# Linear attention with a highway layer: sums of two batches moved earlier, x copies on ScalarE, x added on GpSimd for three of four blocks

## The chip, the cores and the metric

The kernel runs on one core of a Trainium2 chip. The core has five engines that each work through a queue of their own: TensorE (matrix products; PE in the profile, its weight loads PEld), VectorE (DVE), ScalarE (ACT), GpSimd (POOL) and SyncE (SP, which here issues all the transfers). They wait for one another through semaphores. The metric is the time of one execution on the device, in microseconds (us); less is better. "Before" is the kernel without the change, "after" the one with it.

## The reference

Two layers in a row. The first is linear attention on 8 batches of 8 heads, 576 positions and 64 features: q goes through a softmax over its features, k through a softmax over the positions, and the output is q's softmax times the 64x64 matrix of k's softmax times v. The second is a highway layer with 512 features on the 4608 rows (batch times position) that come out.

```python
def _attn_ref(q, k, v):                       # each (8, 8, 576, 64)
    q_s = softmax of q over axis -1
    k_s = softmax of k over axis 2
    kv = np.einsum('bhsd,bhse->bhde', k_s, v)
    return np.einsum('bhsd,bhde->bhse', q_s, kv)

x = attn_out.transpose(0, 2, 1, 3).reshape(4608, 512)

def _moe_ref(x, w_h, w_t, b_t):
    H = np.maximum(x @ w_h, 0.0)
    T = 1.0 / (1.0 + np.exp(-(x @ w_t + b_t)))
    return T * H + (1.0 - T) * x
```

## The kernel before

**Tiles.** A batch's q, k and v are loaded as 128 partitions x 4 head pairs x 9 position groups x 64 features in fp32. The 9 groups are split as 4 + 4 + 1 where transposes are concerned; eight of the nine make a "row block" of 512 columns, and the ninth groups of all batches are gathered in `x9` for the end.

**The chain of a batch b.** ScalarE takes the exponential of q and of k, each in two halves (`exp_half`, line 170). VectorE sums q's exponential over the features, in two halves (`q_sums`, line 225), and takes the reciprocal (`q_recip`, line 243). GpSimd multiplies the exponential by it (`q_scale_p`, line 255, tile `eq`), in two parts, and casts v to fp16 (`cast_v`, line 182). TensorE transposes the scaled q (`q_trans`, line 67, tile `pq`; copied to SBUF as `qsT` by VectorE, line 272) and multiplies k by v in two halves (`kv_half`, tile `psk`); v carries a column of ones, so that k's sums come out beside it. VectorE divides by these sums (`kv_norm`, lines 212 and 214, tile `kvn`). TensorE then makes x, the attention's output in transposed form (`x_pair`, tile `px`, four blocks of 128 features), and ScalarE or VectorE copies it to SBUF as `xT` (lines 295 and 297). The ninth group goes its own way (`x_left`, line 310).

**The highway layer of a row block c** (c = b; blocks 8 and 9 are the two halves of `x9`) has four output blocks `ob`. For each, TensorE makes the gate's product (`gate`, tile `pt`), on which ScalarE puts a tanh (line 332), and the carry product (`carry`, tile `ph`, with half the weight less the identity). VectorE makes `dd` (line 350) and the blend `g` (`blend`, line 358). Then x has to be added. For blocks in `added(g)` GpSimd does it (`add_x`, line 367); for the others TensorE does it for nothing but its own time, by transposing x into the same PSUM tile as `g`, in `turn_block`. An output tile (`out_tile`, tile `nat`) turns one position group of two row blocks, g = c // 2, back into rows: for each of four feature blocks one matmul with `g` as the weights, and one more with `xT` where GpSimd didn't add. ScalarE copies it (line 397), and SyncE stores four tiles at a time (line 400).

**What sets the order.** The kernel is scheduled by hand. The list at the end (line 515) gives the order of the start. After it, each piece of work is entered with a due time by `at(p, ...)`, where a row block takes 8 units, and all pieces are emitted in the order of their times; pieces with the same time, in the order of entry. Each engine keeps the order in which its instructions were emitted. Batch b's preparation stands in row block b - 1 (p = 8 * (b - 1)) and, for the exponential and the sums of q, in the block before that one. The numbers in lines 477 to 511 are what the change touches:

```python
    for b in range(2, B):
        p = 8 * (b - 1)
        ...
        for i in range(3):
            at(p + tr[i], E(q_trans, b, i))
        at(p + kv[0], E(kv_half, b, 0))
        at(p + kv[1], E(kv_half, b, 1), E(kv_norm, b))
        at(p + x[0], E(x_pair, b, 0))
```

**Buffers.** PSUM has four tiles for `pt` and `ph`, three (`ps_q`) for `pq`, `psk` and `px`, and one for `nat`. SBUF has two of each exponential, three of `xT`, two of `g`, three of each loaded tensor.

Of the kernel before, what the change touches and what calls it, by code (L numbers as in the profile page):

```python
# [18 lines left out]
def kernel(  # L19
# [10 lines left out]
    nc = tc.nc  # L30
# [3 lines left out]
    N9 = S // 64  # L34
# [239 lines left out]
    def x_pair(b, a, even=False, home=None):  # L274
        ps, tag = home or (ps_q, "qx")
        g, b2 = b // 2, b % 2
        if a == 0 and b2 == 0:
            xT[g] = xtp.tile([P, 4, NM, 2, 64], FP16, tag="xT", name=f"xT_{g}")
        t = [
            ps.tile([P, NM, 64], FP32, tag=tag, name=f"px_{b}_{a}_{c}")  # L280
            for c in range(2)
        ]
        for x in range(2):
            for c in range(2):
                r = slice(64 * c, 64 * c + 64)
                mm(
                    t[c][64 * x : 64 * x + 64].rearrange("p n d -> p (n d)"),
                    kvn[b % 2][r, x, a, :],
                    qsT[b][r, 2 * a + x, 0:NM, :].rearrange("p n d -> p (n d)"),
                    True, True,  # L290
                )
        for c in range(2):
            dst = xT[g][:, 2 * a + c, :, b2, :]
            if (c == 0) if even else (a + c < 2):
                nc.scalar.copy(dst, t[c])  # L295
            else:
                nc.vector.tensor_copy(dst, t[c])  # L297
# [62 lines left out]
        )  # L360


    added = lambda g: (0, 1) if g < 3 else (0, 1, 2)

    def add_x(c, ob):
        xv, gv = views(c)
# [71 lines left out]
    def at(p, *fs):  # L438
        events.setdefault(p, []).extend(fs)

    E = lambda f, *a: (lambda: f(*a))

    for c in range(1, B + 2):
        for ob in range(4):
            p = 8 * c + 2 * ob
# [6 lines left out]
    for g in range(B // 2):  # L452
        p = 16 * (g + 1)
# [6 lines left out]
    p = 8 * B + 8  # L460
# [10 lines left out]
    at(14.5, E(add_x, 1, 1))  # L471
    for c in range(2, B):
        for ob in added(c // 2):
            at(8 * c + 2 * ob + 2.5, E(add_x, c, ob))
    at(11, E(cast_v_head, 2, 2, nc.gpsimd), E(cast_v_head, 2, 3, nc.scalar))
    at(11, E(q_scale_p, 2, 8, N9))
    for b in range(2, B):
        p = 8 * (b - 1)
        if b > 2:
            s = p + {3: -2, 4: -4}.get(b, -5)  # L480
            at(s, E(exp_half, b, "q", 0))
            at(s + 1, E(exp_half, b, "q", 1))
            if b > 3:
                at(s + 1, E(q_sums, b, 0))
                at(s + (3.5 if b == 4 else 2), E(q_sums, b, 1), E(q_recip, b))
            else:
                at(s + 2.5, E(q_sums, b, 0))
                at(s + 3.5, E(q_sums, b, 1), E(q_recip, b))
            if b > 3:
                at(s + (3.6 if b == 4 else 2), E(q_scale_p, b, 0, 4))  # L490
                at(s + (3.7 if b == 4 else 3), E(q_scale_p, b, 4, N9))
            s = p + {3: 0, 4: 0}.get(b, -1)
            at(s, E(exp_half, b, "k", 0))
            at(s + 1, E(exp_half, b, "k", 1))
            s -= 2 if b == 4 else 0
            at(s, E(cast_v, b, 0))
            at(s + 1, E(cast_v, b, 1))
            if b == 3:
                at(p + 1.6, E(q_scale_p, b, 0, 4), E(q_scale_p, b, 4, N9))
        tr, kv, x = {  # L500
            2: ((5, 6, 6.4), (4, 6.2), (7, 7.5, 7.6)),
            3: ((4.5, 5.5, 6), (3, 4), (6.5, 7, 7.5)),
            4: ((2, 3, 4), (4, 5), (6, 6, 7)),
        }.get(b, ((2, 3, 4), (3, 4), (5, 6, 7)))
        for i in range(3):
# [4 lines that stand above are left out]
        at(p + x[1], E(x_pair, b, 1))  # L510
        at(p + x[2], E(x_left, b))
    for b in range(4, B):
        at(8 * (b - 3), *[E(load, b, w) for w in "qkv"])

    for f in [
        E(warm_up, 20),
        E(exp_half, 0, "q", 0), E(q_sums, 0, 0),
        E(exp_half, 0, "q", 1), E(q_sums, 0, 1),
        E(q_recip, 0), E(q_scale_v, 0, 0, 4), E(q_scale_v, 0, 4, N9),
        E(exp_half, 0, "k", 0), E(cast_v, 0, 0),  # L520
        E(exp_half, 0, "k", 1), E(cast_v, 0, 1),
        E(q_trans, 0, 0), E(q_trans, 0, 1), E(warm_up, 2), E(q_trans, 0, 2),
        E(warm_up, 6),
        E(kv_half, 0, 0), E(gate_bias), E(warm_up, 2), E(kv_half, 0, 1), E(kv_norm, 0),
        *[E(cast_weight, "t", k_, (nc.vector, nc.gpsimd)[k_ % 2]) for k_ in range(4)],
        E(warm_up, 4),
        E(x_pair, 0, 0), E(warm_up, 2), E(x_pair, 0, 1), E(warm_up, 1), E(x_left, 0),
        E(exp_half, 1, "q", 0), E(q_sums_tree, 1, 0),
        E(exp_half, 1, "q", 1), E(q_sums_tree, 1, 1), E(q_recip, 1),
        E(less_one, 0), E(cast_weight, "h", 0, nc.scalar, 0.5),  # L530
        E(less_one, 1), E(cast_weight, "h", 1, nc.gpsimd, 0.5),
        E(less_one, 2), E(cast_weight, "h", 2, nc.scalar, 0.5),
        E(less_one, 3), E(cast_weight, "h", 3, nc.scalar, 0.5),
        E(q_scale_p, 1, 0, 4), E(q_scale_p, 1, 4, 8),
        E(gate, 0, 0), E(gate, 0, 1), E(gate, 0, 2, (ps_q, "qx")), E(warm_mid, 5),
        E(carry, 0, 0), E(blend, 0, 0), E(carry, 0, 1), E(exp_half, 1, "k", 0),
        E(gate, 0, 3, (ps_nat, "nat")), E(blend, 0, 1), E(carry, 0, 2),
        E(q_trans, 1, 0), E(blend, 0, 2), E(carry_products, 0, 3),
        E(exp_half, 1, "k", 1),
        *[E(cast_v_head, 1, c, (nc.scalar, nc.gpsimd, nc.gpsimd, nc.scalar)[c]) for c in range(4)],  # L540
        E(q_scale_p, 1, 8, N9),
        *[E(load, 2, w) for w in "qk"], E(load, 2, "v", [nc.sync, nc.sync]),
        *[E(load, 3, w) for w in "qkv"],
        E(q_trans, 1, 1), E(kv_half, 1, 0), E(kv_half, 1, 1), E(kv_norm, 1),
        E(q_trans, 1, 2), E(carry_diff, 0, 3), E(exp_half, 2, "q", 0),
        E(x_pair, 1, 0, True), E(x_pair, 1, 1, True, (ps_ht, "ht")),
        E(q_sums_tree, 2, 0), E(exp_half, 2, "q", 1), E(q_sums_tree, 2, 1), E(q_recip, 2),
    ]:
        f()
# [33 lines left out]
```

The softmax here doesn't subtract the row's maximum and nothing guards it: scores larger than these inputs give would overflow.

## Time and profile before

| | |
|---|---|
| median of 5 runs | 136.52 us (135.57 to 136.84) |
| the profiled execution: its time, its span | 136.79 us, 134.9 us |
| TensorE busy | 116.0 us, 86% of the span |
| VectorE busy | 104.6 us, 78% |
| ScalarE busy | 90.7 us, 67% |
| GpSimd busy | 71.2 us, 53% |
| granted TensorE clock | 0.999 |
| read from HBM, written | 30.41 MB, 9.44 MB |

The page cuts the span into 40 slices of 3.4 us, each digit the busy share in tenths:

```profile
PE   4949996897798698787797999899989999999960
DVE  1395638599998798978599788988998775779880
ACT  3651256989955798569669869796975566566630
POOL 2006419960399929966934983499089632430000
DMA  4999999999999999984999399993007004227874
```

The first six slices are the start: batch 0 is loaded and goes through its chain. From about 43 us on (slice 13) the blocks follow each other: row block 2 has its gates from 46 us, block 3 from 60, block 4 from 74, block 5 from 86, block 6 from 98, block 7 from 110. TensorE is nearly always busy there[...]. The end, from 118 us on, has no attention left: blocks 8 and 9 and the last tiles.

### The profile page before, as it was taken

The page shows a single profiled execution, that of the slowest core. Times are in us where ns is not written, and L with a number is a line of the kernel's source. Part 1 is how long each engine was busy: PE and PEld are TensorE (multiplying, and loading weights), DVE is VectorE, ACT ScalarE, POOL GpSimd, SP SyncE. Part 2 cuts the span into 40 slices and gives each one's busy share as a digit, 9 for nine tenths or more (in the row PEclk, how much of TensorE's full clock was granted, in tenths as well). Part 3 has the DMA queues.
Part 4 walks back from the last instruction along what each step waited for, and adds up shares of the span by engine and source line. Part 5 has one row for each costly group of instructions (what it writes and reads, how often), then busy time and mean ns, then how long its engine had stood idle before and what let it go on. Part 6 is the DMA issues. An engine that isn't in the chain of part 4 may idle for free.

```text
span 134.9 us, 3493 instructions
## 1 busy us (share of the span) xinstructions
PE 116.0 (86%) x1427; PEld 64.5 (48%) x1427; DVE 104.6 (78%) x209; ACT 90.7 (67%) x134; POOL 71.2 (53%) x65
## 2 busy tenths in 40 slices
PE   4949996897798698787797999899989999999960
PEld 1425341362354255444452564456446555589950
DVE  1395638599998798978599788988998775779880
ACT  3651256989955798569669869796975566566630
POOL 2006419960399929966934983499089632430000
PEclk9999999999999999999999999999999999999999
DMA  4999999999999999984999399993007004227874
GB/s 140 374 389 373 412 402 411 412 412 410 406 413 400 412 411 415 401 334 177 279 411 410 151 281 401 404 422 134 0 0 316 2 0 199 117 95 323 357 313 160
DMA packets 15847, 40.06 MB, mean 297 GB/s; under 512 B 724, under 2 KB 1240, under 8 KB 14808
## 3 DMA queue, kind: packets, MB, share of 16 engines
q1 hardware_dynamic: 15832, 39.85, 76.6%
q8 instruction: 11, 0.18, 0.5%
q14 instruction: 4, 0.03, 0.1%
HBM read 30.41 MB, written 9.44 MB: 295 GB/s over the span
## 4 chain that ended last, share of the span: by engine, by line
PE 43%; DVE 20%; ACT 9%; POOL 8%; DMA 8%; SPq 6%; issue 3%; DVEq 0%; ACTq 0%; POOLq 0%
PE pt L62 14%; PE ph L62 12%; DMA w32h<-in_moe_w_h_dram 8%; PE nat L62 6%; POOL eq L255 6%; PE pq L67 4%; DVE r L225 4%; DVE dd L350 4%; SPq L94 4%; DVE g L358 3%; PE psk L62 3%; ACT pt L332 3%; ACT ek L170 3%; DVE xT L297 2%; SPq L109 2%
## 5 line engine op out<-in xcount | busy, mean ns | idle before, releaser
L255 POOL TENSOR_TENSOR eq<-eq,r 128x1024 f16<-128x1024 f16 (+2 forms) x16 | 29.7, 1875 | 17.6 <-DVE r L243 11.0
L332 ACT ACTIVATE pt<-pt,bt 128x512 f32<-128x512 f32 (+1 forms) x40 | 24.7, 622 | 21.2 <-PE pt L62 21.2
L62 PE MATMUL pt<-xT,w16t 128*128 128x512 f16 x128 | 33.4, 380 | 2.2 <-DVE xT L297 0.9
L62 PE MATMUL ph<-xT,w16h 128*128 128x512 f16 x128 | 33.3, 380 | 1.5 <-ACT w16h L114 1.0
L350 DVE SCALAR_TENSOR_TENSOR dd<-xT,ph 128x512 f16<-128x512 f16 x32 | 21.9, 684 | 7.4 <-PE ph L62 6.5
L358 DVE SCALAR_TENSOR_TENSOR g<-pt,dd 128x512 f16<-128x512 f32 (+1 forms) x40 | 25.0, 627 | 2.3
L367 POOL TENSOR_TENSOR g<-g,xT 128x512 f16<-128x512 f16 x18 | 20.5, 1153 | 9.3 <-DVE g L358 9.3
L170 ACT ACTIVATE eq<-q 128x1152 f16<-128x1152 f32 x16 | 18.5, 1171 | 4.5 <-DMA q<-in_q_dram 4.5
L62 PEld LDWEIGHTS <-w16t 128*128 128x128 f16 x160 | 14.1, 98 | 14.4 <-issue 3.2
L62 PEld LDWEIGHTS <-w16h 128*128 128x128 f16 x160 | 13.7, 98 | 12.7 <-ACT w16h L114 2.2
L170 ACT ACTIVATE ek<-k 128x1152 f16<-128x1152 f32 x16 | 18.5, 1171 | 1.6 <-DMA k<-in_k_dram 1.6
L225 DVE TENSOR_REDUCE r<-eq 128x18 f32<-128x1152 f16 x12 | 16.2, 1346 | 3.8 <-ACT eq L170 3.7
L182 POOL CAST v<-v 128x1152 f16<-128x1152 f32 x12 | 13.5, 1148 | 9.9 <-DMA v<-in_v_dram 9.9
L295 ACT CAST xT<-px 128x512 f16<-128x512 f32 x23 | 12.8, 594 | 7.8 <-PE px L62 7.8
L397 ACT COPY o<-nat 128x512 f32<-128x512 f32 x28 | 16.6, 594 | 1.9 <-PE nat L62 0.9
L62 PE MATMUL nat<-ident,g 128*128 128x128 f16 x142 | 17.6, 219 | 0.2
L62 PEld LDWEIGHTS <-g 128*128 128x128 f16 x144 | 13.7, 98 | 7.8 <-issue 1.4
L67 PE MATMUL pq<-ident,eq 128*128 128x128 f16 x144 | 12.0, 219 | 5.7 <-POOL eq L255 2.9
L272 DVE COPY qsT<-pq 128x1024 f16<-128x1024 f16 (+1 forms) x24 | 13.2, 554 | 3.6 <-PE pq L67 3.3
L67 PEld LDWEIGHTS <-eq 128*128 128x128 f16 x144 | 9.2, 98 | 9.7 <-POOL eq L255 4.1
L62 PE MATMUL warm<-wide,ident 128*128 128x512 f16 x37 | 10.6, 429 | 1.8 <-DVE wide L151 1.8
L62 PE MATMUL nat<-ident,xT 128*128 128x128 f16 x56 | 9.7, 219 | 0.0
(50 smaller groups left out, 104.4 us busy)
## 6 DMA issues: line engine op xcount, KB each, us to landing
out_dram<-o SPq DMA_DIRECT2D x8, 1024.0 KB, 5.1
q<-in_q_dram SPq DMA_DIRECT2D x7, 1152.0 KB, 13.8
k<-in_k_dram SPq DMA_DIRECT2D x7, 1152.0 KB, 13.2
v<-in_v_dram SPq DMA_DIRECT2D x5, 1152.0 KB, 13.7
v<-in_v_dram SPq DMA_DIRECT2D x6, 576.0 KB, 11.8
q<-in_q_dram SPq DMA_DIRECT2D x2, 576.0 KB, 4.0
k<-in_k_dram SPq DMA_DIRECT2D x2, 576.0 KB, 6.9
w32t<-in_moe_w_t_dram SPq DMA_DIRECT2D x1, 1024.0 KB, 10.7
```

What stands on the lines that cost most here:

```text
L62: mm = lambda o, l, r, st, sp: nc.tensor.matmul(o, l, r, start=st, stop=sp, skip_group_check=True)
L67: nc.tensor.matmul(o, i, ident, is_transpose=True, start=True, stop=True, skip_group_check=True,)
L170: nc.scalar.activation(dst[b][:, :, 2 * a : 2 * a + 2, :], in32[which][b][:, 2 * a : 2 * a + 2].rearrange("p c n d -> p n c d"), AF.Exp,)
L182: (eng or nc.gpsimd).tensor_copy(o, i)
L225: nc.vector.reduce_sum(qsum[b][:, :, h], eq[b][:, :, h, :], axis=AX.X)
L255: nc.gpsimd.tensor_mul(e, e, r.broadcast_to(list(e.shape)))
L272: nc.vector.tensor_copy(qsT[b][:, :, n0:n1, :], t[:, :, 0:w, :])
L332: nc.scalar.activation(ps, ps, AF.Tanh, bias=bt2[:, ob : ob + 1], scale=0.5)
L350: nc.vector.scalar_tensor_tensor(dd, xv(ob), -0.5, ps, op0=ALU.mult, op1=ALU.max)
L358: nc.vector.scalar_tensor_tensor(gv(ob), th, 1.0, dd, op0=ALU.add, op1=ALU.mult)
L367: nc.gpsimd.tensor_add(gv(ob), gv(ob), xv(ob))
L397: nc.scalar.copy(o, flat(t))
```

## The change

It moves work between engines and along the order, in five places:

- **x copies.** For batches 3 to 7, the fourth block of x is copied to SBUF by ScalarE, like the other three; before, VectorE copied it (5 copies).
- **x added.** For the row blocks 2 to 5, GpSimd adds x for three of the four feature blocks; before, for two. TensorE's output tiles of these rows take five matmuls each, not six (16 fewer in all). The third addition is emitted at 8 c + 7.4, which on GpSimd is behind the scaling of batch c + 2 and ahead of its v.
- **Start.** The second quarter of the carry weight is cast by ScalarE, not by GpSimd, so ScalarE casts all four.
- **Batches 3 and 4.** The exponential of q, its sums, and its scaling come up to a unit and a half earlier. For batch 3 the first half of q is ahead of the tanh of row block 1's last gate on ScalarE, the first sum is ahead of that block's last carry on VectorE, the scaling stands between the two halves of v on GpSimd, and the first transposes come ahead of the second half of k times v. For batch 4 the exponential is ahead of the third tanh of row block 2, the sums are ahead of that block's third carry and third blend, and the scaling is ahead of v.
- **Batches 5 to 7.** The order of exponentials and sums stays; v is emitted half a unit later, behind the third addition.

On each engine the instructions come to: VectorE five fewer, ScalarE six more, GpSimd three more, TensorE 16 matmuls and their weight loads fewer. SyncE's order of transfers is the same.

```diff
-            if (c == 0) if even else (a + c < 2):
+            if (c == 0) if even else (b > 2 or a + c < 2):
                 nc.scalar.copy(dst, t[c])
...
-    added = lambda g: (0, 1) if g < 3 else (0, 1, 2)
+    added = lambda g: (0, 1, 2) if g else (0, 1)
...
         for ob in added(c // 2):
-            at(8 * c + 2 * ob + 2.5, E(add_x, c, ob))
+            at(8 * c + (2.5, 4.5, 7.4)[ob], E(add_x, c, ob))
...
         if b > 2:
-            s = p + {3: -2, 4: -4}.get(b, -5)
-            at(s, E(exp_half, b, "q", 0))
-            at(s + 1, E(exp_half, b, "q", 1))
-            if b > 3:
-                at(s + 1, E(q_sums, b, 0))
-                at(s + (3.5 if b == 4 else 2), E(q_sums, b, 1), E(q_recip, b))
-            else:
-                at(s + 2.5, E(q_sums, b, 0))
-                at(s + 3.5, E(q_sums, b, 1), E(q_recip, b))
-            if b > 3:
-                at(s + (3.6 if b == 4 else 2), E(q_scale_p, b, 0, 4))
-                at(s + (3.7 if b == 4 else 3), E(q_scale_p, b, 4, N9))
-            s = p + {3: 0, 4: 0}.get(b, -1)
-            at(s, E(exp_half, b, "k", 0))
-            at(s + 1, E(exp_half, b, "k", 1))
-            s -= 2 if b == 4 else 0
-            at(s, E(cast_v, b, 0))
-            at(s + 1, E(cast_v, b, 1))
-            if b == 3:
-                at(p + 1.6, E(q_scale_p, b, 0, 4), E(q_scale_p, b, 4, N9))
+            e0, e1, s0, s1, sc = {
+                3: (-2.6, -1.6, -1.1, -0.1, 1),
+                4: (-5.5, -4.5, -3.7, -2.7, -2.6),
+            }.get(b, (-5, -4, -3.9, -2.9, -2.8))
+            at(p + e0, E(exp_half, b, "q", 0))
+            at(p + e1, E(exp_half, b, "q", 1))
+            at(p + s0, E(q_sums, b, 0))
+            at(p + s1, E(q_sums, b, 1), E(q_recip, b))
+            at(p + sc, E(q_scale_p, b, 0, 4), E(q_scale_p, b, 4, N9))
+            s = p + {3: 0, 4: 0}.get(b, -0.5)
+            at(s, E(exp_half, b, "k", 0), E(cast_v, b, 0))
+            at(s + 1, E(exp_half, b, "k", 1), E(cast_v, b, 1))
         tr, kv, x = {
...
-            3: ((4.5, 5.5, 6), (3, 4), (6.5, 7, 7.5)),
+            3: ((4, 5, 5), (3, 4), (6, 7, 7)),
...
-        E(less_one, 0), E(cast_weight, "h", 0, nc.scalar, 0.5),
-        E(less_one, 1), E(cast_weight, "h", 1, nc.gpsimd, 0.5),
-        E(less_one, 2), E(cast_weight, "h", 2, nc.scalar, 0.5),
-        E(less_one, 3), E(cast_weight, "h", 3, nc.scalar, 0.5),
+        *[f for k_ in range(4) for f in (E(less_one, k_), E(cast_weight, "h", k_, nc.scalar, 0.5))],
```

## The prediction

> **What bounds the kernel now.** I read the page's head first: the span is 134.9 us, the profiled run took 136.79 us, so 1.9 us lie around it. No engine is saturated over the span, so the busy shares say little; the waits of TensorE say where it loses time. From the waits (engine and line, what it waited for: us in all, times, longest):
> ```profile
> POOL eq L255 <- DVE r L243: 11.0, 3, 4.0
> PEld L67 <- POOL eq L255: 4.1, 4, 1.3
> PE pq L67 <- POOL eq L255: 2.9, 4, 0.8
> PE px L62 <- ACT xT L295: 1.3, 2, 0.9
> PE pt L62 <- DVE xT L297: 0.9, 2, 0.4
> ```
> GpSimd's scaling of the exponentials (eq, line 255) waits for VectorE's reciprocal, and TensorE's transposes (pq) wait for the scaling. The page's groups give what the change buys on GpSimd:
> ```profile
> L255 POOL TENSOR_TENSOR eq<-eq,r 128x1024 f16<-128x1024 f16 (+2 forms) x16 | 29.7, 1875 | 17.6 <-DVE r L243 11.0
> L367 POOL TENSOR_TENSOR g<-g,xT 128x512 f16<-128x512 f16 x18 | 20.5, 1153 | 9.3 <-DVE g L358 9.3
> L182 POOL CAST v<-v 128x1152 f16<-128x1152 f32 x12 | 13.5, 1148 | 9.9 <-DMA v<-in_v_dram 9.9
> ```
> TensorE's timeline says where the waits lie (start, us, operation, idle before it):
> ```profile
> 63.94 0.62 PE L67 MATMUL pq<-ident,eq 128*128 128x128 f16 x8 [0.84 <-POOL eq L255]
> 66.23 0.62 PE L67 MATMUL pq<-ident,eq 128*128 128x128 f16 x8 [0.81 <-POOL eq L255]
> ...
> 87.05 0.38 PE L62 MATMUL pt<-xT,w16t 128*128 128x512 f16 x1 [0.43 <-DVE xT L297]
> ...
> 99.29 0.38 PE L62 MATMUL pt<-xT,w16t 128*128 128x512 f16 x1 [0.43 <-DVE xT L297]
> ...
> 101.56 0.28 PE L62 MATMUL nat<-ident,g 128*128 128x128 f16 x2
> ```
> Batch 4's scaling costs TensorE two waits near 65 us; then VectorE's copy of x costs 0.43 us a batch; from 77 us on a batch takes 12.25 us, nearly all of it TensorE work. GpSimd beside it:
> ```profile
> 98.26 4.19 POOL L255 TENSOR_TENSOR eq<-eq,r 128x1024 f16<-128x1024 f16 x2 [3.63 <-DVE r L243]
> 102.40 2.24 POOL L182 CAST v<-v 128x1152 f16<-128x1152 f32 x2
> 104.60 2.26 POOL L367 TENSOR_TENSOR g<-g,xT 128x512 f16<-128x512 f16 x2
> ```
> Here GpSimd is in the scaling of batch 7 until 102.4, while TensorE starts the output tile of rows 4/5 (nat) at 101.56. Today that tile needs no GpSimd result that comes after the scaling.
>
> [...]
>
> **The change, part by part.** (Steps back to back: x copy on VectorE 0.60, on ScalarE 0.50; sum 1.26; add 1.13; scaling 1.90+2.29; v half 1.10; gate or carry product 0.87, 0.97 after 64-row matmuls; transpose 0.056.)
>
> *Start.* One weight cast (1.49 us) leaves GpSimd, where it held up two subtractions; ScalarE casts four quarters from 21.33 at 0.53 each, so to 23.46 instead of 24.22 us. The last quarter of the weight lands at about 21.6 and is subtracted by 22.2, in time. Everything behind (tanh, carry, batch 1's and 2's chains) comes 0.75 us sooner. GpSimd's own scaling at 23.56 waits for a reciprocal and gains nothing; it isn't last. Loads have landed: q3 at 38.9, needed at 39; v3 by 45.7 at the latest, needed before 47.
>
> *Batch 3.* Its exponential goes ahead of the last tanh, into ScalarE's 1.9 us gap before 41.0; its first sum fills VectorE's gap near 43. The second follows the copies of x leftovers: 45.6 to 46.9, reciprocal 47.25 (before 50.75), scaling 47.4 to 51.6. But the second half of v now stands behind the scaling: to 52.7, so the second half of k'v, which could start at 51.55, waits 1.15 us. Then VectorE has the normalisation, a sum of batch 4, a carry and the transposed copy in a row, and x waits 0.55 us more, to 56.4. The block ends where it would with the start's gain alone (gates of row block 3 at 58.95 instead of 59.66, -0.7): batch 3's old waits (0.42, 0.81) are traded for these.
>
> *Batch 4.* Exponentials behind the first output copy, from 50.5; sums at 53.9 and 56.5, reciprocal 58.15 (before 61.81), scaling 58.3 to 62.5. TensorE reaches the transposes at 62.25 and 63.55: both waits go, 2.0 us. v4, behind the scaling and one add, is done at 64.7 and 65.8; needed 65.3 and 66.7. SyncE's order is the same; batch 6's loads stand behind the first output store, which waits for ScalarE's copy of the fourth tile, 0.9 us sooner. Fewer VectorE copies give 0.15 more. Gain here: recip of batch 5 at 69.85 instead of 72.62, -2.77.
>
> *x copies.* Five leave VectorE (batches 3 to 7, 5 x 0.60), five come to ScalarE (5 x 0.50), where they end before the gate's last matmul needs them: the two 0.43 us waits go. They stand ahead of the exponential of k, which has over 2 us of slack.
>
> *Adds.* Four more on GpSimd (4.5 us), 16 x-transposes fewer on TensorE (16 x 0.056 = 0.9, of which some half are hidden by waits below). The new third add of a block stands behind the next-but-one batch's scaling and ahead of its v. This price I take from GpSimd's order:
> - Block 3: reciprocal 69.85 + 0.17 + 4.19 + 1.13 = 75.3; the output tile of rows 2/3 could start at 74.2. Wait 1.05.
> - Batch 6: reciprocal 83.75 (before 85.86); scaling, add, first half of v: 90.3; TensorE is ready at 88.6. Wait 1.75 (against before's block, which had 0.2 us to spare).
> - Block 5: reciprocal of batch 7 at 96.85 (before 98.10); scaling and add to 102.3; TensorE reaches the tile at 99.65. Wait 2.65.
>
> Behind each waiting tile stand the next transposes and carry product, ScalarE's copy of the tile, and behind that the next exponential of q, so nothing runs ahead. The transposes of batch 7 follow at 102.5; before they started at 101.89. So the whole lead of 2.8 us is spent and 0.6 is lost; the seven tiles after it win back 7 x 0.056 = 0.4. From 102 to 118 us TensorE has no gap today, and the end isn't touched. Sum: +0.2 us on the profiled 136.79, that is 137.0. The median of the runs shown is 136.52, 0.27 lower, so I put the forecast at 136.7 on their scale.
>
> Unknown costs: an x copy more on ScalarE could make nothing late or cost 0.1 us a batch (0 to +0.5, I take 0). A hop from GpSimd to TensorE shows 0.06 us; three of them at up to 0.2 make +0.4 at most, and a wait cannot gain (0). GpSimd beside VectorE: its add was 1.15 us in every place, so 0. Batch 3's two new waits come out of my sums over eight steps: from 0 (both hidden, -1.7) to double (+1.7); I take 1.7 as worked out.
>
> **The rivals.**
> *Faster: batch 3's waits don't come.* If the half of v is cast in time and the sums find room, x of batch 3 starts at 54.7 instead of 56.4, and the lead of every reciprocal behind it grows by 1.7: 135.0 us. For it: the scaling is 3.5 us sooner, and VectorE idles 0.4 and 0.8 us near 44 in this trace. Against: GpSimd's order puts v behind the scaling, which is fixed.
> *Slower: GpSimd's loop decides from batch 5 on, and the lead isn't there.* From reciprocal to reciprocal a batch now takes 4.36 (hop and scaling) + 1.13 + 1.1 + 2.3 (k'v and what lies between) + 4.3 (normalisation to reciprocal) = 13.1 us, against 12.25. That loop and the last tile cost 3.3 us in all, whatever happens before. If a load binds the start (k2 lands at about 33.0 and would be needed at 33.9, so from 0.9 us later on), its 0.75 is gone: 137.5; if batch 3's order costs another 0.9 as well, 138.4. For it: the DMA engines are at nine tenths until 57 us. Against: of v1 to v4 only v2 was waited for here.
> *Slower, by the clock.* [...]
>
> **How the numbers follow.** I give the forecast (gain and loss cancel, 136.0 to 137.4) 0.38, the faster rival 0.28, the loop without the lead 0.28 and the clock 0.06. What this kernel's measurement can tell from no change is about 0.5%, 0.7 us. So faster 0.28, same 0.38, slower 0.34. The range 134.9 to 138.3 leaves out a tenth on either side; the forecast's own is 136.0 to 137.4.
>
> **What would show it.** Right: waits of the nat loads for the add (L367) of about 1.0 and 2.6 us, one of k'v for v (L182) near 1.7 us, none of pq for eq after 60 us; reciprocals of batches 5, 6 and 7 earlier by 2.8, 2.1 and 1.3 us; carry products starting 0.75 us sooner. Wrong: nat tiles that don't wait (then the lead stays and it is near 134), or a reciprocal of batch 5 less than 2 us sooner (then slower).

## The result, and the profile after

The kernel with the change takes 138.63 us in the median of 21 runs (137.09 to 140.39), the kernel before 136.56 us in the median of 40 runs. The ratio of comparable runs is 1.010, with an interval of 1.0075 to 1.013: about 1% slower. (Executions more than 1.5% above the fastest of the same kernel are left out of ratios as disturbed; here that takes out part of what the change does, so the medians of all runs stand further apart, at 1.015.) On the scale of 136.52 the ratio gives 137.9 us, inside the predicted range of 134.9 to 138.3; the medians of all runs would give 138.6, just outside it. The forecast itself, 136.7 us and no change, was too low by 1.2 us.

The runs of after are not one cluster. Beside each time stands TensorE's mean granted clock in that execution:

| mean granted clock | runs | time, us |
|---|---|---|
| 0.998 to 1.0 | 7 | 137.09 to 137.39, and 137.8 |
| 0.984 to 0.986 | 5 | 138.16 to 139.01 |
| 0.971 to 0.975 | 9 | 139.17 to 140.39 |

So after costs 0.5% at full clock (a mean of 0.998 to 1.0), and up to 2.8% otherwise. First the full clock: the profiled run (137.8 us, span 136.1 us, clock 0.998) is one of these, and the slowest of them. In its waits (engine and line, what it waited for: us in all, times, longest) the waits for the scaling are all but gone and waits for the third addition and for v have come:

```profile
POOL eq L255 <- DVE r L243: 14.9, 6, 3.9
...
PE nat L62 <- POOL g L367: 3.2, 2, 2.4
PE psk L62 <- POOL v L182: 3.0, 2, 1.6
...
PE pt L62 <- ACT xT L295: 1.6, 1, 1.6
...
PEld L67 <- POOL eq L255: 0.3, 1, 0.3
```

The page's groups: GpSimd has four more additions, at the same duration each, and ScalarE 28 copies of x; TensorE's busy time fell from 116.0 to 114.3 us.

```profile
L367 POOL TENSOR_TENSOR g<-g,xT 128x512 f16<-128x512 f16 x22 | 25.1, 1155 | 8.9 <-DVE g L358 8.9
...
L295 ACT CAST xT<-px 128x512 f16<-128x512 f32 x28 | 15.2, 595 | 8.8 <-PE px L62 8.7
```

TensorE's timeline (start, us, operation, idle before it) puts the new waits in their places:

```profile
32.03 1.08 PE L62 MATMUL pt<-xT,w16t 128*128 128x512 f16 x4 [1.59 <-ACT xT L295]
...
52.59 0.48 PE L62 MATMUL psk<-v,ek 64*64 64x65 f16 x36 [1.45 <-POOL v L182]
...
56.32 0.41 PE L62 MATMUL px<-qsT,kvn 64*64 64x512 f16 x4 [0.53 <-DVE qsT L272]
...
75.42 0.23 PE L62 MATMUL nat<-ident,g 128*128 128x128 f16 x1 [0.81 <-POOL g L367]
...
90.59 0.48 PE L62 MATMUL psk<-v,ek 64*64 64x65 f16 x36 [1.58 <-POOL v L182]
...
102.63 0.23 PE L62 MATMUL nat<-ident,g 128*128 128x128 f16 x1 [2.42 <-POOL g L367]
...
102.81 0.61 PE L67 MATMUL pq<-ident,eq 128*128 128x128 f16 x8
```

And GpSimd's, beside the last of them. Where the tile of rows 4/5 needed nothing after the scaling before, it now waits for the addition that follows it:

```profile
97.28 4.19 POOL L255 TENSOR_TENSOR eq<-eq,r 128x1024 f16<-128x1024 f16 x2 [3.43 <-DVE r L243]
101.43 1.14 POOL L367 TENSOR_TENSOR g<-g,xT 128x512 f16<-128x512 f16 x1
102.52 2.23 POOL L182 CAST v<-v 128x1152 f16<-128x1152 f32 x2
```

How the lead comes and goes, read from the same timelines of both kernels: first carry result (dd of block 0) 23.48 instead of 24.80 us, reciprocal of batch 5 done at 69.90 instead of 72.62, of batch 6 at 83.97 instead of 85.86, of batch 7 at 97.12 instead of 98.10, and the transposes of batch 7 start at 102.81 instead of 101.89. A lead of 2.7 us has turned into a lag of 0.9 us. VectorE's last work ends 0.8 us later than before. All of this is in one execution at full clock, and not a quick one: the second half of batch 0's q landed late, so that batch 0's own reciprocal, ahead of everything that was changed, is done at 9.57 instead of 8.66 us. The run "two adds, filled" below, which had no such delay, has the reciprocal of batch 5 at 69.42 us. So after's usual lead there is probably nearer to 3.2 us.

The first of the waits, at 32.03 us, is one that the prediction doesn't have. ScalarE's timeline (same columns) shows whence it comes:

```profile
30.34 1.16 ACT L170 ACTIVATE eq<-q 128x1152 f16<-128x1152 f32 x1 [1.84 <-DMA q<-in_q_dram]
31.41 1.05 ACT L295 CAST xT<-px 128x512 f16<-128x512 f32 x2
```

The exponential of q of batch 2 waits for its load, which lands at 30.3 us; the copies of x stand behind it in ScalarE's queue, and TensorE's gates of block 1 wait for these. With the start 1.3 us later, as before, the same queue cost TensorE 0.46 us.

### The profile page after: what moved, and what is told of

It is laid out like the page before. It is cut to its first block, busy times and chain, and to the rows that moved or that the text cites. A ratio compares the mean times of both kernels' runs of the same rounds, so it can differ in the third digit from the quotient of the medians.

```text
span 136.1 us, 3467 instructions
## 1 busy us (share of the span) xinstructions
PE 114.3 (84%) x1411; PEld 64.2 (47%) x1411; DVE 100.5 (74%) x204; ACT 93.3 (69%) x140; POOL 74.1 (54%) x68
## 4 chain that ended last, share of the span: by engine, by line
PE 30%; DVE 23%; DMA 18%; POOL 13%; issue 5%; ACT 3%; SPq 3%; POOLq 0%; DVEq 0%
DMA q<-in_q_dram 18%; PE ph L62 9%; POOL eq L255 9%; PE pt L62 9%; DVE r L225 7%; PE nat L62 5%; DVE dd L350 5%; DVE g L358 3%; PE pq L67 3%; SPq L94 3%; POOL g L367 2%; PE psk L62 2%; PE px L62 2%; POOL v L182 2%; ACT eq L170 2%
## 5 line engine op out<-in xcount | busy, mean ns | idle before, releaser
L62 PE MATMUL pt<-xT,w16t 128*128 128x512 f16 x128 | 32.7, 380 | 1.8 <-ACT xT L295 1.6
L62 PE MATMUL ph<-xT,w16h 128*128 128x512 f16 x128 | 32.8, 380 | 0.0
L367 POOL TENSOR_TENSOR g<-g,xT 128x512 f16<-128x512 f16 x22 | 25.1, 1155 | 8.9 <-DVE g L358 8.9
L295 ACT CAST xT<-px 128x512 f16<-128x512 f32 x28 | 15.2, 595 | 8.8 <-PE px L62 8.7
L62 PE MATMUL nat<-ident,g 128*128 128x128 f16 x142 | 17.1, 219 | 3.5 <-POOL g L367 3.2
L272 DVE COPY qsT<-pq 128x1024 f16<-128x1024 f16 (+1 forms) x24 | 13.1, 553 | 7.4 <-PE pq L67 7.0
L62 PEld LDWEIGHTS <-g 128*128 128x128 f16 x144 | 13.1, 98 | 10.2 <-POOL g L367 3.6
L62 PE MATMUL warm<-wide,ident 128*128 128x512 f16 x37 | 11.1, 445 | 1.8 <-DVE wide L151 1.8
L62 PE MATMUL psk<-v,ek 64*64 64x65 f16 x576 | 7.7, 194 | 3.3 <-POOL v L182 3.0
```

What stands on the lines that cost most here:

```text
L62: mm = lambda o, l, r, st, sp: nc.tensor.matmul(o, l, r, start=st, stop=sp, skip_group_check=True)
L367: nc.gpsimd.tensor_add(gv(ob), gv(ob), xv(ob))
```

## The experiments

The theory after this: (1) the third additions give back the lead that the rest of the change wins, through the three waits for GpSimd; (2) what lies above 137.2 us comes from TensorE's clock, which falls behind its new gaps (waits in which TensorE stands idle). The rivals: the lead was never there; the clock falls for a reason of its own. All differences below are against the kernel before, measured on the same chip, unless another kernel is named.

**Two adds.** The third additions taken out again, all else as in after.

```diff
-    added = lambda g: (0, 1, 2) if g else (0, 1)
+    added = lambda g: (0, 1) if g < 3 else (0, 1, 2)
```

> The changed kernel, but GpSimd adds x for two blocks of four in row blocks 2 to 5, as before (everything else stays changed). Theory (the third add stands behind a 4.19 us scaling and in front of v, and TensorE waits 0.8, 1.6 and 2.4 us for it): these waits go, the lead of 2.8 us at batch 5's reciprocal is kept, and the copy of x no longer costs 0.43 us a batch; batch 7's transposes start near 98.3 us instead of 102.8, and the time is 133.4 us, a ratio of 0.977 to before. Rival (the other four edits cost the time, the adds are worth their 0.9 us of TensorE): the time rises by up to 0.9 us over the changed kernel, to 138 us or more.

134.3 us (133.56 to 135.94), ratio 0.982 (0.979 to 0.986). At full clock 133.56 and 133.66 us, 3.7 us less than the 137.29 that after takes in the median at full clock: the lead is real and the additions spend it. But the runs at 0.973 to 0.981 took 134.5 to 135.9 us, although the long gap at 100 us is gone; so that gap wasn't the only cause of the low clock.

**Third adds alone**, on the kernel before, with v half a unit later as they need it.

```diff
-    added = lambda g: (0, 1) if g < 3 else (0, 1, 2)
+    added = lambda g: (0, 1, 2) if g else (0, 1)
-            at(8 * c + 2 * ob + 2.5, E(add_x, c, ob))
+            at(8 * c + (2.5, 4.5, 7.4)[ob], E(add_x, c, ob))
...
+            s += 0.5 if b > 4 else 0
             at(s, E(cast_v, b, 0))
```

> The kernel before with the third add alone (at 8 c + 7.4, and v of batches 5 to 7 half a unit later, so that GpSimd's order from batch 5 on is the changed kernel's). Theory: no lead at batch 5's reciprocal (72.6 us), then the same loop; TensorE waits about 1, 1.3 and 2.4 us for GpSimd and the end is 2.5 to 3 us later than before: 139.3 us at full clock, a ratio of 1.02, more where the clock falls. Rival (the adds save 16 matmuls and cost little): 135.7 to 136.5 us.

139.98 us (139.08 to 140.9), ratio 1.025 (1.020 to 1.029): 3.5 us slower, with the profiled run at clock 1.0. The price of the additions is about the same with and without the other parts.

**Start undone.** After with the old casts of the carry weight.

```diff
-        *[f for k_ in range(4) for f in (E(less_one, k_), E(cast_weight, "h", k_, nc.scalar, 0.5))],
+        E(less_one, 0), E(cast_weight, "h", 0, nc.scalar, 0.5),
+        E(less_one, 1), E(cast_weight, "h", 1, nc.gpsimd, 0.5),
+        E(less_one, 2), E(cast_weight, "h", 2, nc.scalar, 0.5),
+        E(less_one, 3), E(cast_weight, "h", 3, nc.scalar, 0.5),
```

> The changed kernel, but GpSimd casts the second quarter of the carry weight at the start, as before. Theory (a lead at the start runs through batch 3's reciprocal into the GpSimd loop and moves the end by itself): 0.75 us longer than the changed kernel at the same granted clock, about 138.0 us at full clock. Rival (the loop on GpSimd sets the end from batch 5 on and takes up an early lead): no change, 137.2 us at full clock.

139.16 us (138.26 to 140.82), ratio 1.018 (1.014 to 1.022). The one run at full clock, 138.26, is 1.0 us above after's median at full clock; another, at 0.996, took 139.37. The traces show less: in the profiled run the reciprocal of batch 5 is done at 69.85 us, beside after's 69.90 with its late load, and 69.42 in "two adds, filled". The profiled run (clock 0.986) also shows a fall of the clock. TensorE in windows of time (window, its length, TensorE's busy us and instructions, granted clock, share of DMA, GB/s):

```profile
100.00:103.00 3.00, 0.58 (x8) 0.93 0.83 350
103.00:106.00 3.00, 3.00 (x19) 0.50 0.00 0
106.00:109.00 3.00, 3.00 (x91) 1.00 0.03 8
```

In the window at 100 us TensorE is busy for 0.58 of 3.0 us, waiting for the addition (2.42 us); in the next it runs at half its clock: the four carry matmuls behind the wait take 1.91 us together, and 1.03 us in after. (The counts of instructions can't be compared, as the windows hold matmuls of different sizes.) The clock of 0.93 in the first window would put the fall at about 102.6 us, an estimate that takes the low clock as 0.50 throughout. The profiled run of after has the same gap, of 2.42 us, and a clock of 1.00 in all three windows: the gap doesn't cost the clock every time. Why it did in the one execution and not in the other isn't shown.

**Gaps filled.** After, with matmuls whose result is overwritten in the three waits for GpSimd. They add work only where TensorE would wait, so a gain points to the clock.

```diff
+        for _ in range({(1, 0): 4, (2, 0): 11}.get((g, n), 0)):
+            mm(t.rearrange("p k d -> p (k d)"), ident, wide, True, True)
         for k_ in range(4):
             turn_block(
...
+            for _ in range(7 if b == 6 else 0):
+                mm(psk[b][0].rearrange("p a d -> p (a d)"), ident, wide, True, True)
```

> The changed kernel with matmuls whose result is overwritten, put where TensorE waits: 4 ahead of the first output tile of rows 2/3, 7 ahead of batch 6's k'v, 11 ahead of the first output tile of rows 4/5 (0.216 us each, so that each stretch is a little shorter than its wait or about as long). The wait's end stays where it is. Clock theory (the idle gap [...]is where the times of 138 to 140 us with a mean granted clock of 0.97 to 0.985 come from): granted clock 0.998 or more in every execution, median about 137.3 us, no times over 138.5. Rival (the low clock has nothing to do with the gaps): the same spread as the changed kernel, 137.1 to 140.4 us with clocks down to 0.97, and a median near 138.5.

137.76 us (136.98 to 139.38), ratio 1.010 (1.0065 to 1.014): half of what theory (2) expected. Seven of 13 runs lie between 136.98 and 137.76 us at 0.99 to 1.0, the other six still between 138.35 and 139.38 at 0.967 to 0.981. The profiled run is one of these, and its windows show another place:

```profile
30.00:33.40 3.40, 2.18 (x38) 0.87 1.05 413
33.40:36.80 3.40, 3.40 (x19) 0.62 1.03 403
...
100.00:103.00 3.00, 3.00 (x15) 1.00 0.50 210
103.00:106.00 3.00, 2.95 (x29) 1.00 0.35 145
```

Nothing at 100 us any more; but at about 32.5 us, at the end of a wait for the copies of x (0.84 us in this execution), the clock falls. In windows of 2 us it is 0.63 from 32 us, 0.51 from 34 and 1.00 from 36, which makes 3.4 us at half clock, an estimate as above.

**All gaps filled.** The same, and seven overwritten matmuls ahead of block 1's first gate.

```diff
         ps = ps.tile([P, rows_of(c), 64], FP32, tag=tag, name=f"pt_{c}_{ob}")
+        for _ in range(7 if (c, ob) == (1, 0) else 0):
+            mm(ps.rearrange("p n d -> p (n d)"), ident, wide, True, True)
```

> The kernel after, with overwritten matmuls in all four of TensorE's gaps: the three waits for GpSimd in the loop (as in the fill of gaps before) and the wait of 1.59 us for the xT copies at 32 us. Theory A (after's executions run from 137.2 to 140.4 us because TensorE's granted clock falls behind gaps of 1.6 to 2.4 us; the gap at 32 us is the second such place): no run shows a mean clock below 0.99, the slices behind 32 us and behind 100 us are all at 1.0, and the median is 137.2 us, ratio 1.005. Rival B (the clock falls for a reason that has nothing to do with gaps, and the fill of the loop only met it less often): runs at 0.97 to 0.985 remain in about half of the executions, median 138 us or more, ratio 1.010.

137.05 us in ten runs, none outside 136.58 to 137.56; ratio 1.005 (1.003 to 1.0075). The spread of 3.3 us has become one of 1.0 us, and the profiled run shows the same windows full and at full clock:

```profile
30.00:33.40 3.40, 3.40 (x24) 1.00 1.04 406
33.40:36.80 3.40, 3.16 (x49) 1.00 1.04 411
...
100.00:103.00 3.00, 2.96 (x24) 1.00 0.63 265
103.00:106.00 3.00, 3.00 (x94) 1.00 0.03 8
```

One run still has a mean clock of 0.983, at 137.53 us. (A mean a little under 1.0 can come from the end alone: in the profiled run of after, 0.998, the clock is 1.00 up to the last matmul, which ends at 131.6 us, and falls to 0.50 at 135.58 us.) This is shown, then: most of the loss of clock comes in the filled gaps, and without it the change costs 0.5%. The share of each gap isn't shown, and a rest remains that these gaps don't explain. Of the 22 runs of the three kernels with filled gaps (this one and two below) four are under 0.99, and so are 5 of the 17 runs of before in the same session, three of these at 138.0 to 139.4 us. One further place was caught, in the profiled run of "the start alone" below (137.09 us): the clock, 0.92 from 8 to 12 us, is 0.50 from 12 to 14, behind a wait of 2.1 us of the first transposes, and that run took 1.4 us longer than the others of its kernel. Before and after have the same wait, of 1.95 and 2.38 us, nothing filled it, and both profiled runs have a clock of 1.00 from 8 to 16 us.

**Two adds, filled; two adds, copies first.** The gap at 32 us without the additions, once with the seven matmuls of the last experiment, once with its cause removed: the copies of x ahead of the exponential that waits for its load.

```diff
-        E(q_trans, 1, 2), E(carry_diff, 0, 3), E(exp_half, 2, "q", 0),
+        E(q_trans, 1, 2), E(carry_diff, 0, 3),
         E(x_pair, 1, 0, True), E(x_pair, 1, 1, True, (ps_ht, "ht")),
-        E(q_sums_tree, 2, 0), E(exp_half, 2, "q", 1), E(q_sums_tree, 2, 1), E(q_recip, 2),
+        E(exp_half, 2, "q", 0), E(q_sums_tree, 2, 0), E(exp_half, 2, "q", 1), E(q_sums_tree, 2, 1), E(q_recip, 2),
```

> Two adds for groups 0 to 2 (134.3 us in the earlier run, 133.6 at full clock), with seven overwritten matmuls in the gap at 32 us. If that gap is what lowers the clock there (theory A): 133.6 us in nearly every run, ratio 0.978, no slice below 1.0 at 30 to 38 us. If the low clock comes from elsewhere (B): a median of 134.3 us or more, ratio 0.983, and low slices in about half of the executions.

> Two adds for groups 0 to 2, with the xT copies of batch 1 on ScalarE ahead of the exp of q of batch 2, which waits for its DMA; the gap of 1.5 us at 32 us then shrinks to about 0.5 us without filler. If the gap costs by the clock alone: 133.6 us in nearly every run, ratio 0.978. If the copies' delay also costs by itself (block 1's gates stand 1.0 us later): 133.0 us or less, ratio 0.974. If the exp, now behind the copies, delays the reciprocal of batch 2 (34.46 us in the run with two adds) and so GpSimd's loop: 134 us at full clock, and the reciprocal after 35.0 us.

133.72 us (133.38 to 134.04), ratio 0.982 (0.979 to 0.9845), and 133.66 us (133.55 to 133.84), ratio 0.981 (0.9785 to 0.9835). Both end at what two adds gave at full clock, and none of their eleven runs goes beyond 134.04, though two of the filled ones have a mean of 0.981. In the second, TensorE's timeline has the gate 1.3 us sooner than after:

```profile
30.72 1.28 PE L62 MATMUL pt<-xT,w16t 128*128 128x512 f16 x4 [0.46 <-ACT xT L295]
```

That brings nothing by itself: the reciprocal of batch 2 starts at 34.77 us instead of 34.46 in two adds, block 1's third gate waits 1.24 us for VectorE (0.25 in after), and the time isn't below the filled kernel's. So the wait cost by the clock, and not by the delay.

**Third adds of even blocks later.** In after, v of batch 6 (and 4) goes ahead of the addition on GpSimd, which removes most of the wait of 1.58 us; once as it is, once with all gaps filled (three matmuls, not seven, ahead of batch 6's k'v, as that wait is shorter).

```diff
-            at(8 * c + (2.5, 4.5, 7.4)[ob], E(add_x, c, ob))
+            at(8 * c + (2.5, 4.5, 7.4 if c % 2 else 9.05)[ob], E(add_x, c, ob))
```

> The kernel after, with the third add of batches 2 and 4 put behind the casts of v on GpSimd's queue, so that batch 6's v comes 1.1 us sooner. If each wait of TensorE for GpSimd is passed on to the end (theory A, the loop is bound by TensorE and GpSimd in turn): batch 6's wait of 1.58 us for v shrinks to about 0.5 us; the third add of batches 2 and 4 has time until the transposes of its group, so 136.2 us at full clock, about 0.8 to 1.1 us less than after at the same clock. Rival B (that wait only moves: the next one, 2.4 us of the transposes for the adds, grows by as much, because the reciprocal of batch 7 and so GpSimd's work behind it doesn't come sooner): the transposes' wait is 3.4 us, and the time is that of after within 0.3 us at the same clock.

> The kernel with the third add of batches 2 and 4 behind the casts of v (137.3 to 138.3 us with the low clock coming and going, one run of 137.4 at full clock), with overwritten matmuls in the gaps at 32 us, before the first transposes of the second and third group, and three ahead of batch 6's k'v. Compared with the kernel after with all its gaps filled (137.05 us). Theory A (batch 6's 1.1 us are won through to the end, and what hid them was the clock): about 136.0 us, ratio 0.997. Rival B (they are lost again in the next wait, of the transposes for the add of batch 5): 137.0 us, ratio 1.005.

As it is, 137.62 us (137.31 to 138.33), ratio 1.010 (1.007 to 1.0135), no better than after's 137.29 at full clock and not the 136.2 expected. Its profiled run has the wait for v at 0.47 us and the clock low at both places (0.50 from 32 to 34 us, 0.56 from 103 to 106); GpSimd's scaling of batch 5 starts 0.63 us later than in after (70.70 against 70.07), behind the low stretch at 32 us, and that of batch 7 0.47 us sooner (96.81 against 97.28): 1.1 us are won between them, and a second low stretch follows at 103 us. Filled, 136.16 us (135.88 to 136.46), ratio 0.997 (0.993 to 1.001), 0.9 us below after with all its gaps filled. So the wait for v is passed on to the end, and is not merely moved into the next one. One run of the unfilled kernel took 137.4 us with a clock read as 1.0; why that one isn't near 136.2 stays open, and with it whether all that the filling gains there comes from the clock.

**v of batch 3 ahead of its scaling**, on two adds with copies first.

```diff
-                3: (-2.6, -1.6, -1.1, -0.1, 1),
+                3: (-2.6, -1.6, -1.1, -0.1, 1.05),
```

> Two adds, xT copies of batch 1 first (133.66 us), and the second half of batch 3's v on GpSimd ahead of the scaling of its q instead of behind it. Theory A (the wait of 1.45 us of batch 3's k'v at 51 us is passed on to the end): the wait is gone, the scaling ends 0.7 to 1.1 us later, which TensorE's transposes of it (starting 1.4 us after its first half is done) don't feel, and the time is 132.3 us, ratio 0.969. Rival B (the transposes or the x products of batch 3 then wait for the later scaling): a wait of about 1 us for eq or qsT takes its place, 133.4 us or more.

132.31 us (132.06 to 133.5), ratio 0.970 (0.965 to 0.974). GpSimd casts both halves of v first, and TensorE's k'v no longer waits:

```profile
44.52 2.25 POOL L182 CAST v<-v 128x1152 f16<-128x1152 f32 x2
46.87 4.19 POOL L255 TENSOR_TENSOR eq<-eq,r 128x1024 f16<-128x1024 f16 x2
```

```profile
50.67 0.48 PE L62 MATMUL psk<-v,ek 64*64 64x65 f16 x36
...
54.58 0.41 PE L62 MATMUL px<-qsT,kvn 64*64 64x512 f16 x4 [0.70 <-DVE qsT L272]
```

Batch 4's scaling starts at 56.57 us instead of 58.19, and of these 1.6 us 1.35 arrive at the end. This is the fastest kernel of the study: 3% below before.

**x copies undone**, and **the start alone.** The first puts the x copies of batches 3 to 7 back on VectorE, in two adds with copies first; the second is the kernel before with the four casts on ScalarE and the copies first.

```diff
-            if (c == 0) if even else (b > 2 or a + c < 2):
+            if (c == 0) if even else (a + c < 2):
```

> Two adds, xT copies of batch 1 first (133.66 us), with one of the four xT copies of batches 3 to 7 back on VectorE. If the move to ScalarE gains because VectorE's chain to the reciprocal bounds the loop (the prediction took 0.43 us for each batch that it frees ahead of the reciprocal, where GpSimd's work stands behind it): up to 1 us slower, 134.0 to 134.7 us. If it does nothing, because the copy then stands in ScalarE's queue instead: 133.7 us within 0.3 us.

> The kernel before with only the start changed (all four casts of the weight on ScalarE) and the xT copies of batch 1 ahead of the exp of q of batch 2. The start's part was put at 0.75 us by the prediction and measured as 1.0 us at full clock by undoing it in after; if it runs through to the end in the kernel before as well: 135.6 us, ratio 0.993. If the later batches of the kernel before take it up again (batch 3's or 4's GpSimd work waiting for VectorE's sums anyway): 136.5 us, ratio 1.000.

134.37 us (134.11 to 135.53), ratio 0.985 (0.9805 to 0.989): the copies gain 0.7 us (134.37 - 133.66), and TensorE's timeline without them has the two old waits of 0.43 us again, at 97.16 us and here:

```profile
84.92 0.38 PE L62 MATMUL pt<-xT,w16t 128*128 128x512 f16 x1 [0.43 <-DVE xT L297]
```

The start alone: 135.7 us (135.59 to 137.09), ratio 0.995 (0.990 to 0.9997); 0.9 us less than the 136.63 of before in the same session (0.7 us by the ratio, whose interval nearly reaches 1). The copies of batch 1 moved with it; in two adds, moving them gained nothing at full clock.

The parts together, by medians with little or no loss of clock: start -0.9, x copies -0.7, third additions +3.3 (all gaps filled, 137.05, less two adds filled, 133.72). Batches 3 and 4 weren't run alone; by difference they gain 1.3 us (135.7 - 133.66 = 2.0, less 0.7 for the copies). The sum is +0.4 us; all gaps filled against before gives +0.5. As one part is a difference, that agreement is no test of the parts.

## Why the prediction was right, and where it was not

**Right: the sum of gain and loss without the clock.** Forecast +0.2 us; with the gaps filled +0.5, and the seven runs of after at full clock give +0.7 (median 137.29). The mechanism is the one told: a lead built up to batch 5 and spent at three places of GpSimd's queue. Both rivals about the lead fall: batch 3's waits came, and the lead was there.

That the sum came out so near is in part luck. The gains that the text names come to 3.8 us (0.75, 2.0, 0.15 and twice 0.43) and measured 3.0 (136.63 - 133.66); for a sum of +0.2 the additions would have to cost 4.0, and they cost 3.3. Both sides were put too high by about as much. The text's other account, 3.3 us for GpSimd's loop and the last tile, given under the slower rival, is the one that the additions' price agrees with.

- *Start:* put at 0.75 us, measured 0.9 alone (0.7 by the ratio).
- *Batch 3:* the waits of k'v and of x, put at 1.15 and 0.55 us, are 1.45 and 0.53; block 3's gates start at 58.90 us (forecast 58.95). The reciprocal was done at 47.09 us (forecast 47.25). That these waits hold back everything behind them is shown by the run with v ahead; the text counted their removal at 1.7 us, with the wait of x, and left it there, as GpSimd's order is "fixed" in this change. Another order is possible: the wait of x stays, at 0.70 us, and 1.35 us are to be had.
- *Batch 4 and the reciprocals:* both waits of the transposes are gone, put at 2.0 us; batches 3 and 4 together are worth 1.3 by difference. Batches 5, 6 and 7 have their reciprocals at 69.90, 83.97 and 97.12 us (forecast 69.85, 83.75 and 96.85). That these agree to 0.3 us is luck in part too, as that execution had a late load at its start. From one to the next are 14.07 and 13.15 us, where the text has 13.1 for the loop (its terms add up to 13.2).
- *x copies:* the two waits of 0.43 us put in the sum; 0.7 us measured.
- *Adds:* the three waits, put at 1.05 (its terms give 1.1), 1.75 and 2.65 us, are 0.81, 1.58 and 2.42. Against that, the transposes of batch 7 stand at 102.81 us (forecast 102.5), and the tiles behind them won back 0.1 us up to the gates of block 8 and not 0.4: the 16 matmuls less are worth less than their time.

**Wrong: the clock.** The forecast gave "slower, by the clock" a chance of 0.06, the author's estimate. The trace of before has no fall ahead of the last matmul: the mean granted clock is 0.999, and 0.50 comes only from 134.61 us on. Measured: a gap of 2.42 us was followed by a clock of 0.50 in the profiled run of start undone, and 14 of 21 runs of after have a mean clock below 0.99; how these share between the gaps isn't known, as they left no trace. The group at 0.985 lies 1.3 us above full clock. One and the same gap cost the clock in one execution and not in another, and neither the forecast nor the runs say what decides it.

**Missing: the second place.** The start was worked out up to the carry products and taken to bring "everything behind" 0.75 us sooner. The next load on the way wasn't asked: q of batch 2 doesn't come sooner, and ScalarE waits for it with the copies of x behind. The text looked at k2, q3 and v3. The wait cost no time by itself, but it brought a fall of the clock in some executions: in the profiled one with two adds (0.54 from 32 to 34 us, behind a wait of 1.5 us), and perhaps in two more of its six, going by their clocks (0.973 and 0.981).

## What to carry to other kernels

Work put onto an engine that is half idle costs by its place in the queue: four additions of 1.15 us on GpSimd, behind a scaling of 4.19 us and ahead of what TensorE needs, cost 3.3 us, though GpSimd was busy for 54% of the span. Ask for each moved instruction what stands ahead of it, and what the earlier start of a stage will wait for next. And if a kernel's runs fall into groups, look at the granted clock of each run and, slice by slice, behind each gap of TensorE; a few overwritten matmuls in the gap help to tell the clock's share from the wait's.

## What the runs showed of the hardware

- TensorE's granted clock fell to half behind waits of 2.42 us (start undone, 0.50 from 103 to 106 us), 1.5 us (two adds, 0.54 from 32 to 34 us), 2.1 us (the start alone, 0.50 from 12 to 14 us), 1.6 and 2.42 us (even blocks' third adds later, 0.50 from 32 to 34 and 0.56 from 103 to 106 us), and in the profiled run of gaps filled at the end of one of 0.84 us (0.63 from 32 to 34 us), where the work ahead of it was 64-row matmuls. Whether the wait or the work ahead of it counts there wasn't separated.
- With waits of the same sizes the clock also stayed: in after's profiled run it is 1.00 behind 2.38, 1.59 and 2.42 us, in before's behind 1.95 us.
- Each of these six low stretches comes to 3.40 to 3.44 us if the clock in it is taken as 0.50, an estimate from the windows: in the run with even blocks' third adds later, 0.93, 0.50 and 0.72 in the three windows of 2 us from 30 us make 0.28 + 2.0 + 1.12 = 3.40 us, and 0.56 and 0.87 in the two of 3 us from 103 us make 2.64 + 0.78 = 3.42 us.
- The same kernel lost the clock in some executions and not in others: 14 of the 21 runs of after have a mean clock below 0.99. By an estimate from these 3.4 us, one such stretch lowers the mean over a span of 136.1 us by 0.0125, so the table's groups at 0.985 and 0.973 (medians 138.61 and 139.35 us, against 137.29) would be runs with one and with two such stretches; those runs left no trace, so that count is worked out and not seen.
- With seven overwritten matmuls of 512 columns in the gap at 32 us and eleven in the one at 100 us the profiled run (all gaps filled) kept the clock at both places, 1.00 from 30 to 40 and from 97 to 109 us, and the filling cost nothing: 137.05 us, against 137.29 for after at full clock.
